# Values of one pair of blocks and scores of the next pair in one stage, at the ends of groups of units

## The chip, the cores and the metric

The kernel runs on one core of one Trainium2 chip. The metric is the device time of one execution in microseconds (us); the kernel before takes 741.47 us, the median of three runs (741.28 to 741.74).

A core has five engines, each with its own instruction queue: TensorE (PE in the profile; PEld is its weight load), VectorE (DVE), ScalarE (ACT), GpSimd (POOL) and SyncE (SP), which here issues the DMAs. They meet only through semaphores. TensorE writes its results to PSUM, eight banks of 128 x 512 fp32 each, and VectorE or ScalarE must read a bank out before it is written again.

## The reference

A retention block feeds a maxout feed-forward network (FFN):

```python
scores = scale * np.matmul(q, k.transpose(0, 1, 3, 2))        # 8 batches, 8 heads, 576 positions, 64 wide
Dmat = np.where(rel >= 0, gamma[:, None, None] ** rel[None, :, :], 0.0)
attn_out = np.matmul(scores * Dmat[None], v)                  # causal, with a decay per head, no softmax
x = attn_out.transpose(0, 2, 1, 3).reshape(B * S, H * D)      # 4608 tokens x 512
h = np.maximum(np.maximum(x @ w1, x @ w2), x @ w3)            # 512 x 768 each
out = h @ w_out                                               # 768 x 512
```

## The kernel before

**Tiles.** The 4608 tokens are 36 blocks of 128 (`g`, 0 to 35) and nine tiles of 512 (`t`, 0 to 8), four blocks to a tile. Because the decay has no softmax, retention is computed block by block with a running state per head: within a block scores and values, between blocks a 64 x 64 state for each head. From block 8 on (`BY_CHUNKS`) a block is cut into two halves of 64 tokens, so all its matmuls are 64 x 64 and four of them fit in the array at once.

**Retention of a pair of blocks.** For blocks a and b in turn:

- `load` (L244) issues the DMAs on SP: 8 for q and 8 for k in a layout for transposing (L240), then k and v as they lie (L258). `decay` (L260) queues eight scalings of v on ScalarE (L208), which the FFN's loop takes one by one with `scale`.
- `transposes` (L274) queues two VectorE transposes, of k and of q (shown at L213, the line of `chore`).
- `scores` (L297) first issues all that is queued, then calls `chunk_scores` (L369): matmuls `sk` (L376) and `kv` (L379) into two PSUM banks a block, four for a pair, from the pool `ps_r`, which has four. It queues the causal mask (L383) and the updates of the state (L391 to L397, with a GpSimd multiply at L393 between two of them).
- `values` (L444) calls `chunk_values` (L519): matmuls `o` (L526 from the masked scores, L533 from the state) into two banks, also from `ps_r`, and `chunk_output` queues the two VectorE multiplies that move them into `xT`. At the end of a tile of four blocks `sums_of_x` queues thirteen more VectorE sums, which the FFN of that tile needs.

"Queued" here means put in the Python list `urgent`. While `ffn` runs it issues one entry of it after each fourth matmul, and entries of `chores` (sums of weights, of hidden values) in between. What is issued then stands in the engine's own queue in that order.

**FFN of a tile.** From tile 1 on the FFN uses a bilinear scheme with fewer products. The hidden size is cut into three groups (`fp`). In `up` (L878) a group takes 20 products (`PRODUCTS`), each of two matmuls 128 x 128 x 256 (four records in the profile), summed in five chains A to E. A and B lie in the two banks of `ps_x`; E, C and D take the two banks of `ps_y` in turn. After a product `after` (L886) copies the bank on ScalarE (L890) and joins it to others on VectorE (L893, "joins"). The last four products of a group are D2 (the 17th), B6, A6 and A7; D2, B6 and A7 have three joins each, and A7's finish the hidden values `h` of the group.

After three groups, 120 matmul steps, the down phase runs 20 products (`DOWNS`), numbered here 1 to 20: in `downs` (L719) chains E and G share one bank of `ps_y`, I has the other, H and C share one of `ps_x`, F and D the other. First come ten VectorE sums of `h` (L573). Chain I (`di`) takes product 1 and every second or third one after it, and ScalarE copies its running sum out after most of them (L739). VectorE computes the totals (L573), which both free banks and give the results: y11 reads E's bank after product 7, y14 reads H's bank after product 11; G's product 13 and C's product 15 write to those banks next. Eight results of 128 x 256 leave through a pool of four buffers and a DMA each (L744).

**What sets the order.** The last loop of the kernel runs `ffn(t)` as a generator which yields twelve times: nine times in the three groups (each third of a group, so the third, sixth and ninth yields fall at the ends of groups), after the fourth and tenth down product, and at its end. `steps(t + 1)` lists what is issued of the next tile's retention before each yield; `at(n, ...)` puts an entry at place n, so place 3, 6 and 9 are ends of groups, and 10 lies inside the down phase:

```python
        for n in range(0, CPT, 2):
            a, b, m = CPT * t + n, CPT * t + n + 1, 6 * (n // 2)
            ...
            at(s, (scores, a), (scores, b), (load, b + 2))
            at(s + 1, (decay, a + 2))
            at(s + 2, (decay, b + 2))
            at(s + 3, (values, [a, b]), (transposes, a + 2), (load, a + 4))
```

So for each tile scores of the first pair stand at place 1, its values at 4, scores of the second pair at 7 and its values at 10. A "visit" below is one such stay of TensorE at the 64 x 64 matmuls, between large ones. "Call t" is `steps(t)`.

## Time and profile before

| | before |
|---|---|
| median of three runs | 741.47 us |
| the profiled execution, first to last instruction (span) | 739.6 us |
| TensorE busy | 734.1 us, 99% |
| VectorE busy | 576.1 us, 78% |
| ScalarE busy | 345.0 us, 47% |
| GpSimd busy | 33.8 us, 5% |
| granted TensorE clock, mean | 0.999 |
| one tile's FFN with the next tile's retention (355 to 433 us) | 78.0 us |
| in it: TensorE, VectorE, ScalarE busy | 78.0, 58.9, 36.2 us |
| waits of TensorE in its list | 2.2 us, at the start |

In rows of the timeline the first number is the start in us from the span's start, the second the time from the first start to the last end, then engine, line, operation, the tile written and the tiles read, partitions x elements, and how many instructions the row merges. A bracket gives idle time before it and what ended that. The ends of matmuls are modelled, so a stream of them is read by its starts. A row of waits names who waited for whom. An L2xx line of VectorE's work may be the line of the helper that issued it (L208 scalings, L213 entries of `urgent`).

### The profile page before, as it was taken

The page shows a single profiled execution, that of the slowest core. Times are in us where ns is not written, and L with a number is a line of the kernel's source. Part 1 is how long each engine was busy: PE and PEld are TensorE (multiplying, and loading weights), DVE is VectorE, ACT ScalarE, POOL GpSimd, SP SyncE. Part 2 cuts the span into 40 slices and gives each one's busy share as a digit, 9 for nine tenths or more (in the row PEclk, how much of TensorE's full clock was granted, in tenths as well). Part 3 has the DMA queues.
Part 4 walks back from the last instruction along what each step waited for, and adds up shares of the span by engine and source line. Part 5 has one row for each costly group of instructions (what it writes and reads, how often), then busy time and mean ns, then how long its engine had stood idle before and what let it go on. Part 6 is the DMA issues. An engine that isn't in the chain of part 4 may idle for free.

```text
span 739.6 us, 17315 instructions
## 1 busy us (share of the span) xinstructions
PE 734.1 (99%) x6948; PEld 605.8 (82%) x6948; DVE 576.1 (78%) x1066; ACT 345.0 (47%) x731; POOL 33.8 (5%) x42
## 2 busy tenths in 40 slices
PE   8999999999999999999999999999999999999998
PEld 7654556888888888888888888888888888888887
DVE  5998897999886895699668876787768966893676
ACT  4674824454245534544354525543455255424441
POOL 2000000102000100000000000000100010000000
PEclk9999999999999999999999999999999999999999
DMA  9999533415242515141424243332514151000001
GB/s 209 249 245 268 116 59 83 89 21 96 66 85 42 97 36 105 39 83 44 109 51 75 49 107 60 59 58 58 115 22 95 39 106 30 1 31 29 0 1 57
DMA packets 226640, 58.85 MB, mean 80 GB/s; under 512 B 207872, under 2 KB 225280, under 8 KB 226560
## 3 DMA queue, kind: packets, MB, share of 16 engines
q1 hardware_dynamic: 225584, 57.71, 35.8%
q8 instruction: 54, 0.88, 0.5%
q14 instruction: 26, 0.21, 0.1%
q10 hardware_dynamic: 976, 0.04, 0.1%
HBM read 48.27 MB, written 9.44 MB: 78 GB/s over the span
## 4 chain that ended last, share of the span: by engine, by line
PE 97%; SPq 1%; DMA 1%; DVE 0%; issue 0%
PE a L905 20%; PE b L905 17%; PE c L905 9%; PE up L930 8%; PE di L750 7%; PE d L905 6%; PE e L905 6%; PE dhc L750 5%; PE deg L750 3%; PE sk L376 3%; PE down L917 3%; PE o L526 2%; PE dfd L750 2%; PE o L533 2%; PE dx L657 1%; SPq L258 1%
## 5 line engine op out<-in xcount | busy, mean ns | idle before, releaser
L893 DVE TENSOR_TENSOR part<-part 128x512 f32<-128x512 f32 x168 | 117.8, 701 | 86.2 <-ACT part L890 83.6
L890 ACT COPY part<-b 128x512 f32<-128x512 f32 x120 | 70.4, 586 | 163.5 <-PE b L905 163.5
L893 DVE TENSOR_TENSOR h<-h,part 128x512 f32<-128x512 f32 x120 | 83.2, 693 | 24.5 <-ACT h L890 20.5
L890 ACT COPY part<-a 128x512 f32<-128x512 f32 x96 | 56.3, 586 | 51.6 <-PE a L905 51.1
L208 ACT ACTIVATE vraw<-vraw,gk 128x64 f32<-128x64 f32 x240 | 76.8, 347 | 0.1
L905 PE MATMUL b<-s,n 128*128 128x256 f32 x288 | 73.9, 379 | 0.0
L930 PE MATMUL up<-xT,w 128*128 128x512 f32 (+2 forms) x160 | 64.2, 554 | 0.0
L905 PEld LDWEIGHTS b<-s,n 128*128 128x128 f32 x288 | 54.7, 190 | 7.4
L930 PEld LDWEIGHTS up<-xT,w 128*128 128x128 f32 x160 | 28.5, 190 | 29.4 <-issue 26.3
L905 PE MATMUL c<-xT,w 128*128 128x256 f32 x192 | 51.2, 389 | 0.0
L739 ACT COPY k<-di 128x256 f32<-128x256 f32 x49 | 18.2, 372 | 68.4 <-PE di L750 43.4
L905 PE MATMUL d<-s,w 128*128 128x256 f32 x192 | 49.8, 380 | 0.0
L905 PE MATMUL a<-xT,w 128*128 128x256 f32 x192 | 49.3, 379 | 0.0
L905 PE MATMUL b<-xT,n 128*128 128x256 f32 x192 | 49.3, 379 | 0.0
L905 PE MATMUL a<-s,w 128*128 128x256 f32 x192 | 49.3, 379 | 0.0
L393 POOL TENSOR_TENSOR s<-s,gs_of 64x512 f32<-64x512 f32 x21 | 22.5, 1072 | 558.1 <-DVE s L391 441.7
L905 PE MATMUL e<-xT,w 128*128 128x256 f32 x192 | 45.4, 379 | 0.0
L905 PE MATMUL a<-xT,n 128*128 128x256 f32 x192 | 45.4, 379 | 0.0
L905 PEld LDWEIGHTS e<-xT,w 128*128 128x128 f32 x192 | 36.5, 190 | 5.4 <-issue 0.5
L905 PEld LDWEIGHTS a<-xT,w 128*128 128x128 f32 x192 | 36.5, 190 | 5.0
L905 PEld LDWEIGHTS a<-s,w 128*128 128x128 f32 x192 | 36.5, 190 | 5.0
L905 PEld LDWEIGHTS b<-xT,n 128*128 128x128 f32 x192 | 36.5, 190 | 5.0
(200 smaller groups left out, 1378.2 us busy)
## 6 DMA issues: line engine op xcount, KB each, us to landing
bits<-in_moe_w_dram SPq DMA_DIRECT2D x36, 256.0 KB, 5.7
kraw<-in_k_dram SPq DMA_DIRECT2D x32, 256.0 KB, 3.1
vraw<-in_v_dram SPq DMA_DIRECT2D x32, 256.0 KB, 3.5
qraw<-in_q_dram SPq DMA_DIRECT2D x224, 32.0 KB, 2.1
kxraw<-in_k_dram SPq DMA_DIRECT2D x224, 32.0 KB, 2.1
out_dram<-osb SPq DMA_DIRECT2D x56, 128.0 KB, 1.7
bits<-in_moe_w_out_dram SPq DMA_DIRECT2D x6, 512.0 KB, 4.9
qraw<-in_q_dram SPq DMA_DIRECT2D x7, 256.0 KB, 5.6
```

What stands on the lines that cost most here:

```text
L208: scaling.popleft()()
L376: nc.tensor.matmul(s[half(c), h, :], lhsT=kT[half(c), h, :], rhs=qT[half(c), h, :], start=True, stop=True)
L393: nc.gpsimd.tensor_tensor(new, new, factor, op=ALU.mult)
L526: nc.tensor.matmul(o[m][half(c), n, u, :], lhsT=vds[g][half(m), h, :], rhs=sts[g][half(m), h, :], start=n == 0 and u == 0, stop=place(g, m ...
L533: nc.tensor.matmul(o[m][half(c), n, u, :], lhsT=stacks[g][half(m), h, :], rhs=qks[g]["q"][half(m), h, :], start=False, stop=True, skip_gro ...
L739: nc.scalar.copy(place, a)
L750: nc.tensor.matmul(banks[chain], lhsT=hidden(h, order, b, late_ones)[:, e], rhs=late["V"][v][:, e], start=begins and e == 0, stop=chain no ...
L890: nc.scalar.copy(of[step], ps[step[0]][:])
L893: nc.vector.tensor_tensor(of[dst], a, b, op=op)
L905: nc.tensor.matmul(ps[chain][:, e, :], lhsT=factor(w, 2 * fp + e), rhs=xS[t][x], start=n == 1 and e == 0, stop=ends, skip_group_check=True)
L917: nc.tensor.matmul(b[:], lhsT=h[:, fb, m * P:(m + 1) * P], rhs=w_sb["out", fb], start=fb == blocks[0], stop=fb == blocks[-1])
L930: nc.tensor.matmul(ps[:, a:b], lhsT=w_sb[i, fb][:, dc * P:(dc + 1) * P], rhs=xT[t][:, dc, a:b], start=dc == 0 and a == 0, stop=dc == NDC - ...
```

## The change

The change adds `merged`, which issues the values of one pair and the scores of the next without large matmuls between; rewrites the lists for calls 2 to 8; lets `chunk_values` take its two banks from `ps_y` instead of `ps_r`; and issues the two output multiplies at once where it does. Values (two banks), and scores of a pair (four), then use six banks in one stage. In call 3 the first pair's scores still stand alone at place 1, and the merged stages at 6 and 9; in calls 4 to 8 they stand at 3 and 9. After the stage both blocks of the pair after next are loaded, at once and not through `urgent`. For tiles from 2 on the flush of both lists moves ahead of the ninth yield. Three buffer counts change: k as it lies, from three (and one beside them) to two (and two), transposed q in halves from three to four, and the tag it shares with early scores with it.

```diff
-            bufs = {"k": 3, "q": 2, "v": 4}[n]
-            pool, bufs = (raw0, 1) if n != "v" and g < BY_PE and g % (bufs + 1) == bufs else (raw, bufs)
+            extra = {"k": 2, "q": 1, "v": 0}[n]
+            pool, bufs = (raw0, extra) if g < BY_PE and g % (2 + extra) >= 2 else (raw, 2)
...
-                both[n] = att.tile([P, H, D], FP32, tag=tag, name=n + "T", bufs=2 if n == "k" else 3)
+                both[n] = att.tile([P, H, D], FP32, tag=tag, name=n + "T", bufs=2 if n == "k" else 4)
...
-    def chunk_values(chunks, t, i):
-        o = [ps_r.tile([P, 2, NP, D], FP32, tag="r", name="o") for _ in range(2)]
+    def merged(chunks, following, to_fetch):
+
+        chore(len(urgent))
+        scale(len(scaling))
+        chunk_values(chunks, *divmod(chunks[0], CPT), ps_y, "y")
+        for g in following:
+            if g < NG:
+                chunk_scores(g)
+        for g in to_fetch:
+            if g < NG:
+                load(g)
+
+    def chunk_values(chunks, t, i, pool=ps_r, tag="r"):
+        o = [pool.tile([P, 2, NP, D], FP32, tag=tag, name="o") for _ in range(2)]
...
-        chunk_output(o, chunks, t, i)
+        chunk_output(o, chunks, t, i, pool is ps_y)
...
-            soon(partial(nc.vector.tensor_tensor, x[:, :, :, m], o[m][:],
-                         gq[:, :, half(m)].unsqueeze(1).to_broadcast([P, 2, NP, D]), op=ALU.mult))
+            step = partial(nc.vector.tensor_tensor, x[:, :, :, m], o[m][:],
+                           gq[:, :, half(m)].unsqueeze(1).to_broadcast([P, 2, NP, D]), op=ALU.mult)
+            step() if now else soon(step)
...
                 count += 1
+                if count == total and t > 1:
+                    chore(len(urgent) + len(chores))
...
-        chore(len(urgent) + len(chores))
         if t == 1:
+            chore(len(urgent) + len(chores))
...
-        for n in range(0, CPT, 2):
...
+        if t == 2:
...
+            at(5, (values, [a, b]), (transposes, c), (load, e, "v"), (transposes, d))
+            at(7, (scores, c), (scores, d), (load, e, "k"), (load, f))
+            at(8, (decay, e))
+            at(9, (decay, f))
+            at(10, (values, [c, d]), (transposes, e), (load, g, "v"))
+            return todo
+        if t == 3:
+            at(0, (transposes, b))
+            at(1, (scores, a), (scores, b), (load, c, "k"), (load, d))
+            at(2, (decay, c))
+            at(3, (decay, d), (transposes, c))
+            at(4, (transposes, d))
+            at(6, (merged, [a, b], [c, d], [e, f]))
+            at(7, (decay, e), (decay, f))
+            at(8, (transposes, e), (transposes, f))
+        else:
+            at(1, (transposes, c))
+            at(2, (transposes, d))
+            at(3, (merged, [a, b], [c, d], [e, f]))
+            at(4, (decay, e))
+            at(5, (decay, f))
+            at(6, (transposes, e))
+            at(7, (transposes, f))
+        at(9, (merged, [c, d], [e, f], [g, h]))
+        at(10, (decay, g))
+        at(11, (decay, h))
```

Here a to d are the four blocks of the tile that call t prepares, e to h those of the tile after it.

More of the change, by code (lines that the diff above doesn't have):

```diff
@@ L309, in scores @@
         for j in range(2):
-            st = sts[g, j] = att.tile([C, NP, C], FP32, tag=f"m{j}", name="st", bufs=2 + j)
+            st = sts[g, j] = att.tile([C, NP, C], FP32, tag=f"m{j}", name="st", bufs=2 + 2 * j)
             soon(partial(nc.vector.tensor_tensor, st[:], s[j][:],
@@ L534, in chunk_values, with chunk_output @@
                                          rhs=qks[g]["q"][half(m), h, :], start=False, stop=True, skip_group_check=True)
-        chunk_output(o, chunks, t, i)
-    def chunk_output(o, chunks, t, i):
+        chunk_output(o, chunks, t, i, pool is ps_y)
+    def chunk_output(o, chunks, t, i, now=False):
         if i == 0:
@@ L1112, in at @@
             for step, *args in what:
-                if step is values:
+                if step in (values, merged):
                     if args[0][0] < NG:
-                        todo[n].append(partial(values, *args))
+                        todo[n].append(partial(step, *args))
                 elif args[0] < NG:
@@ L1134, in steps @@
             return todo
-        for n in range(0, CPT, 2):
-            a, b, m = CPT * t + n, CPT * t + n + 1, 6 * (n // 2)
-            first_pair = a == BY_CHUNKS
-            s = m + 2 if first_pair else m + 1
-            at(m - (n > 0), (transposes, b))
-            if first_pair:
-                at(m, (decay, b), (load, a + 2), (carry, a))
-            at(s, (scores, a), (scores, b), (load, b + 2))
-            at(s + 1, (decay, a + 2))
-            at(s + 2, (decay, b + 2))
-            at(s + 3, (values, [a, b]), (transposes, a + 2), (load, a + 4))
+        a, b, c, d = range(CPT * t, CPT * t + CPT)
+        e, f, g, h = range(CPT * t + CPT, CPT * t + 2 * CPT)
+        if t == 2:
+            at(0, (transposes, b), (decay, b), (load, c, "v"), (carry, a))
+            at(2, (scores, a), (scores, b), (load, c, "k"), (load, d))
+            at(3, (decay, c))
+            at(4, (decay, d))
+            at(5, (values, [a, b]), (transposes, c), (load, e, "v"), (transposes, d))
[24 more added lines that the diff above has]
+        at(11, (decay, h))
         return todo
```

## The prediction

> **What bounds the kernel now.** First the page's busy shares and the chain that ended last:

> ```profile
> PE 734.1 (99%) x6948; PEld 605.8 (82%) x6948; DVE 576.1 (78%) x1066; ACT 345.0 (47%) x731; POOL 33.8 (5%) x42
> PE 97%; SPq 1%; DMA 1%; DVE 0%; issue 0%
> ```

> TensorE sets the time and waits for nobody (its waits add up to 2.2 us, all at the start). So an edit gains only by making the stream of matmuls shorter, and loses wherever a matmul must wait. Next, the timeline of TensorE around one scores visit and one values visit:

> ```profile
> 359.95 1.03 PE L905 MATMUL a<-s,w 128*128 128x256 f32 x4
> 360.91 0.27 PE L376 MATMUL sk<-qT,kT 64*64 64x64 f32 x2
> ...
> 362.95 1.13 PE L905 MATMUL c<-xT,w 128*128 128x256 f32 x4
> 363.92 1.03 PE L905 MATMUL b<-s,n 128*128 128x256 f32 x4
> ...
> 374.28 1.89 PE L905 MATMUL e<-xT,w 128*128 128x256 f32 x8
> ...
> 379.46 1.03 PE L905 MATMUL a<-s,w 128*128 128x256 f32 x4
> 380.41 1.16 PE L526 MATMUL o<-m,vraw 64*64 64x64 f32 x64
> 381.39 1.11 PE L533 MATMUL o<-qT,s 64*64 64x64 f32 x64
> 382.44 1.13 PE L905 MATMUL c<-xT,w 128*128 128x256 f32 x4
> 383.40 1.03 PE L905 MATMUL b<-s,n 128*128 128x256 f32 x4
> ```

> Four large records (one product) follow each other every 0.863 us. The values visit begins 0.09 late (380.32 expected), c begins 2.12 after 380.32, and its four records take 0.96, not 0.863: a visit costs 2.22. A scores visit costs 2.14 + 0.10. I use 2.23 for both.

> Then VectorE across the end of a group, where 374.28 above is E of the next group:

> ```profile
> 372.50 2.15 DVE L893 TENSOR_TENSOR part<-part 128x512 f32<-128x512 f32 x3 [2.05 <-ACT part L890]
> 374.69 0.69 DVE L893 TENSOR_TENSOR h<-h,part 128x512 f32<-128x512 f32 x1
> 375.30 1.41 DVE L893 TENSOR_TENSOR part<-part 128x512 f32<-128x512 f32 x2
> 376.62 2.20 DVE L893 TENSOR_TENSOR h<-h,part 128x512 f32<-128x512 f32 x3
> 378.86 0.42 DVE L573 TENSOR_TENSOR h<-h 128x256 f32<-128x256 f32 x1
> ```

> This is the line to remember. Nine joins start when ScalarE has copied D2 and depend on each other, so VectorE finishes a group 4.54 us after TensorE has left it (378.82 against 374.28). Call the moment when TensorE leaves a group T. In a down phase (TensorE leaves at 413.25, last join ends at 417.79) it is 4.54 again. Today that tail costs nothing, because what TensorE starts with needs none of it.

> Last, VectorE's work in a down phase and in a scores stage, TensorE's product 15 of the down phase, and GpSimd:

> ```profile
> 421.43 1.28 DVE L213 TENSOR_TENSOR xT<-o,gq 128x512 f32<-128x512 f32 x2
> 426.56 0.42 DVE L573 TENSOR_TENSOR osb<-dhc,k 128x256 f32<-128x256 f32 x1
> ```

> ```profile
> 427.55 1.03 PE L750 MATMUL dhc<-v,h 128*128 128x256 f32 x4
> ```

> ```profile
> 440.31 0.69 DVE L383 TENSOR_TENSOR m<-sk,causal 128x512 f32<-128x512 f32 x1
> 441.03 1.41 DVE L391 TENSOR_TENSOR s<-kv,s 64x512 f32<-64x512 f32 x2
> 442.47 0.69 DVE L383 TENSOR_TENSOR m<-sk,causal 128x512 f32<-128x512 f32 x1
> ```

> ```profile
> 442.61 1.04 POOL L393 TENSOR_TENSOR s<-s,gs_of 64x512 f32<-64x512 f32 x1 [31.98 <-DVE s L391]
> ```

> Product 15 begins 0.57 after the subtraction y14 (426.56 + 0.42) that reads the bank it writes: the smallest slack there.

> **Part 1, visits saved.** In calls t = 3 to 8 (t is the call here) before has 24 visits, 24 x 2.23 = 53.5 us. After has one lone scores visit and 12 merged stages, 11 of them with scores. A merged stage enters and leaves once: 2.12 + 2.14 less 0.2 is 4.06 us from T to the next large product, which is then 0.10 slow. If nothing waited, 11 merges would save 11 x 0.3 = 3.3 us. Bounds: 0.2 each if the 0.1 before the first large product is not saved, so 2.2 to 3.3.

> [...]

> **Part 2, the wait that the merge adds.** The values now lie in the FFN's banks (ps_y). The next user of the first one is E of the next group (or chain I, the first product of the down phase), and it can start only when VectorE has multiplied that bank into xT. That multiply is issued at once, but behind the nine joins on an engine that takes its work in order. So: joins end T + 4.54; the multiply starts T + 4.58 (378.86) and takes 0.68 (half the pair above is 0.64; its group's mean is 0.682): T + 5.26; a release takes some 0.07 (the values end at 382.50, their multiply starts at 382.56): T + 5.35. TensorE was ready at T + 4.06. The second bank follows at T + 5.95, before its user needs it (C comes four products later, the third down product two later), so it is hidden.

> In the changed kernel's own order five stages (the first of t = 4 to 8) have one transpose of q among the nine joins, 0.63 more (two transposes in a row stood at 389.15 and 389.78): T + 5.98. The second stage of t = 3 has three there, and the last is the one its second block's scores need: those start at T + 4.54 + 1.9 = 6.45, take 1.0, and the down phase starts at T + 7.5. All queued behind the waiting matmul is TensorE's, so each wait counts in full.

> Sum: 6 x 5.35 + 5 x 5.98 + 7.5 = 69.5, plus the lone visit 2.23, less 53.5: **+18.2 us**, the saving of part 1 included. Bounds: with the transposes hidden and no release time 12 x 5.26 + 2.23 - 53.5 = +11.8; with the 0.1 slow product each time and another 1 us in t = 3, +20.4.

> **Part 3, the down phase.** Before, values stood after its fourth product and masks were done in the groups. Now the stage before it puts into VectorE's queue 13 sums of x, two masks and four state updates, drained two per product, ahead of the totals that free banks. From T: multiplies until 5.8; ten hidden sums, 3.72 (417.71 to 421.43): 9.5; 12 of the sums of x, ten of them 3.6 in the trace before plus two of 0.34: 13.8; y11 and the last sum of x: 14.5. Product 13 waits for y11 (14.2) but starts only at 5.35 + 12 x 0.863 = 15.7: hidden, 1.5 to spare. Then mask 0.6, two updates 1.4, mask; GpSimd's 1.04 starts 0.17 after the second update (442.44 to 442.61); two more updates end at 19.1; y14 0.4: 19.55. Product 15 would start at 5.35 + 14 x 0.863 = 17.4 and waits 2.1 us. That holds in four stages (t = 4 to 7); in t = 3, one update fewer, from 7.5, some 1.1. The last (t = 8) has no scores. Nothing in the trace before shows this wait; it is worked out from rows. Below: zero, if the masks cost less than the 2.1 (a gain is excluded: the products' own pace is unchanged). Above: 3 each if GpSimd also holds the first update. I take **+9.5**.

> **Part 4, loads.** Two blocks are loaded at once after each stage: 36 issues at some 0.49 (eight q rows took 3.94) instead of 18. The second block's v is issued after 16 of these, about T + 12.7, and lands 3.5 later (median): T + 16.3. ScalarE's first scaling of it stands ahead of the copy that product 16 waits for, which by part 3 starts at 20.4: hidden, 4 to spare; if product 15 didn't wait, 2 to spare. In t = 3 the transposes are late, so q loads only from T, v lands near 21.5 and product 16 waits about 0.7: **+0.7**, between 0 and 3. The output DMAs queue behind these loads on SP (to T + 13.3), still before y11's data (14.2). The buffers traded between pools (k 3 to 2, q 3 to 4) cost nothing while the scores free k a whole group ahead. The flush that moves ahead of the ninth yield issues the same entries after the same product: nothing. Call 2 keeps its four visits in their places; its loads move but v is still on chip two places (11.5 us) before its scaling, longer than 18 issues and a landing, so nothing; if it were late, ScalarE would hold the groups' copies.

> **Sum.** 18.2 + 9.5 + 0.7 = 28.4. The profiled execution spans 739.6; 768.0 after; the median 741.5 stands 1.9 over the span, so 769.9.

> [...]

> **Rivals.** (a) Only the stage's wait: y14 is in time because masks overlap better than in a chain. 741.5 + 11.8 to 20.4, so 753 to 762. For it: 442.47 shows a mask slipped between. Against: 4.6 us of work is put ahead of a row with 0.57 slack.
> (b) The second block's v comes later than T + 20, ScalarE stands still, and product 16 with it: +2 in five down phases, 780, when it is 2 us past the 4 in hand. For it: ScalarE scales in order; against: 4 us to spare.
> (c) Faster: the multiply gets ahead of the tail. If the last join ended by T + 3.3 (4.06 less 0.68 and 0.07), no stage would wait and 3.3 us were saved: 738. Against: 4.54 at both ends shown, and a chain of nine joins that the change leaves as it is.
> (d) Wait and saving cancel, 741: would need joins ending near T + 3.6.

> **Numbers.** Forecast 0.70, (a) 0.14, (b) 0.10, (c) 0.04, (d) 0.02. The likeliest time is 770. The range 756 to 781 takes in most of (a) and (b). A difference of 0.2% (1.5 us) is about what a measurement of this kernel can tell. Faster 0.04, same 0.02, slower 0.94.

> **What would show it.** Right: E and the first down product start 5.3 to 6 after the last a of a group, released by VectorE's xT; product 15 released by osb<-dhc some 2 us late; some 21 + 10 us of waits in TensorE's list, 13 visits instead of 24. Wrong: TensorE waits for nobody, or its wait names ScalarE or a DMA. The prediction breaks if the joins do not run back to back after a stage.

## The result, and the profile after

The changed kernel takes 775.68 us (median of 5 runs, 774.95 to 776.76) against 741.58 us for the kernel before (5 runs, 741.28 to 741.74): a ratio of 1.046, 95% interval 1.0448 to 1.0474. Forecast were 770 us, with a range of 756 to 781. The profiled execution spans 774.0 us, 34.4 more than before. The page's busy shares and the chain that ended last, of the changed kernel:

```profile
PE 738.6 (95%) x6948; PEld 610.4 (79%) x6948; DVE 580.9 (75%) x1066; ACT 344.3 (44%) x731; POOL 34.0 (4%) x42
PE 79%; DVE 14%; DMA 2%; issue 1%; SPq 1%; ACT 1%; POOL 0%; DVEq 0%; POOLq 0%; ACTq 0%
```

TensorE issues the same 6948 matmuls, but VectorE now holds 14% of the chain, and TensorE's busy share went from 99 to 95%. What it waits for (columns: total us, number of waits, longest us):

```profile
PE dhc L763 <- DVE osb L586: 8.2, 4, 2.1
PE di L763 <- DVE xT L556: 4.4, 3, 3.0
PE di L763 <- ACT k L752: 4.4, 2, 3.7
PE kv L379 <- issue: 4.3, 5, 1.1
PE sk L376 <- issue: 3.3, 3, 1.5
PE sk L376 <- DVE qT L213: 3.2, 1, 3.2
PE e L918 <- DVE xT L556: 2.7, 4, 1.6
```

The first line is the forecast's part 3, lines two and seven are its part 2. Lines four and five were not foreseen: in eight stages TensorE stands still in the middle of the small matmuls, and the profile names nothing that it waits for. They lie beside the wait of part 2 and are hidden by it in this kernel (the stages with such a gap are as long as those without one); the experiments bring them out.

The end of a group, on TensorE and on VectorE (timeline; start, us, engine, line, operation, shape, count):

```profile
428.69 1.24 PE L918 MATMUL a<-xT,n 128*128 128x256 f32 x5
434.98 1.13 PE L763 MATMUL di<-w_out,h 128*128 128x256 f32 x4 [1.16 <-DVE xT L556]
```

```profile
432.12 2.21 DVE L906 TENSOR_TENSOR h<-h,part 128x512 f32<-128x512 f32 x3
434.24 1.28 DVE L556 TENSOR_TENSOR xT<-o,gq 128x512 f32<-128x512 f32 x2
```

T is 428.69 + 5 x 0.2158 = 429.77 (large matmuls follow each other every 0.2158 us, a quarter of a product). The multiply starts 4.47 after T and the first down product 5.21 after T. From T to the next large product, the twelve stages take, in order, 5.21, 7.44 (t = 3), 5.67, 5.21, 5.67, 5.21, 5.67, 5.21, 5.68, 5.21, 5.67 and 5.21 us: 67.1 together, 69.5 forecast.

The down phase of t = 5, on VectorE and TensorE:

```profile
443.44 0.41 DVE L586 TENSOR_TENSOR osb<-deg,k 128x256 f32<-128x256 f32 x1
...
444.11 0.68 DVE L383 TENSOR_TENSOR m<-sk,causal 128x512 f32<-128x512 f32 x1
444.82 1.41 DVE L391 TENSOR_TENSOR s<-kv,s 64x512 f32<-64x512 f32 x2
446.26 0.69 DVE L383 TENSOR_TENSOR m<-sk,causal 128x512 f32<-128x512 f32 x1
447.47 1.41 DVE L391 TENSOR_TENSOR s<-kv,s 64x512 f32<-64x512 f32 x2 [0.52 <-POOL s L393]
448.91 0.42 DVE L586 TENSOR_TENSOR osb<-dhc,k 128x256 f32<-128x256 f32 x1
```

```profile
446.31 1.03 PE L763 MATMUL di<-w_out,h 128*128 128x256 f32 x4
449.39 1.13 PE L763 MATMUL dhc<-v,h 128*128 128x256 f32 x4 [2.05 <-DVE osb L586]
450.36 1.48 PE L763 MATMUL di<-v,h 128*128 128x256 f32 x4
451.63 1.92 PE L763 MATMUL dfd<-w_out,n 128*128 128x256 f32 x4
```

Masks and state updates stand between y11 (443.44) and y14 (448.91), as worked out, and product 15 waits 2.05 us. The last two rows show something else: these products take 1.3 to 1.7 us instead of 0.863. The clock had fallen. The same in t = 3, where ScalarE stood behind a v that had not landed:

```profile
282.89 0.35 ACT L208 ACTIVATE vraw<-vraw,gk 128x64 f32<-128x64 f32 x1 [4.96 <-DMA vraw<-in_v_dram]
```

```profile
278.84 1.06 PE L763 MATMUL dhc<-v,h 128*128 128x256 f32 x4
283.55 2.08 PE L763 MATMUL di<-v,h 128*128 128x256 f32 x4 [3.65 <-ACT k L752]
```

Busy times by stretch, with the granted clock behind POOL's column:

```profile
283.55:286.95 3.40, 3.40 (x8) 2.77 (x9) 0.43 (x1) 1.29 (x5) 0.00 (x0) 0.50 0.03 9
286.95:289.00 2.05, 2.05 (x11) 1.80 (x11) 0.87 (x3) 0.89 (x4) 0.00 (x0) 1.00 0.18 64
```

The clock records have 0.5 from 283.54 for 3.41 us and from 450.79 for 3.41 us; each costs some 1.7 us. Where the 34.4 us went: stages 67.1 + 12 x 0.1 + 2.23 - 53.5 = 17.0. The down phases of t = 4, 6 and 7 take 19.78 where 17.37 is their length without waits (that of t = 8), so 2.41 for product 15 each, in t = 5 as well, 9.6 together. t = 5's takes 21.38, 1.6 more for the clock; t = 3's takes 23.98, of which 4.9 are waits (4.4 by the list) with what follows them, and 1.7 the clock. That is 34.8, with 0.4 too much.

### The profile page after: what moved, and what is told of

The parts are those of the page before. It is cut to its first block, busy times and chain, and to the rows that moved or that the text cites. A ratio compares the mean times of both kernels' runs of the same rounds, so it can differ in the third digit from the quotient of the medians.

```text
span 774.0 us, 17305 instructions
## 1 busy us (share of the span) xinstructions
PE 738.6 (95%) x6948; PEld 610.4 (79%) x6948; DVE 580.9 (75%) x1066; ACT 344.3 (44%) x731; POOL 34.0 (4%) x42
## 4 chain that ended last, share of the span: by engine, by line
PE 79%; DVE 14%; DMA 2%; issue 1%; SPq 1%; ACT 1%; POOL 0%; DVEq 0%; POOLq 0%; ACTq 0%
PE a L918 17%; PE b L918 15%; PE c L918 8%; PE up L943 8%; PE e L918 6%; PE d L918 5%; PE di L763 5%; DVE part L906 4%; PE dhc L763 3%; DVE h L906 3%; PE down L930 3%; PE deg L763 2%; DVE s L586 2%; PE dfd L763 1%; PE dx L670 1%
## 5 line engine op out<-in xcount | busy, mean ns | idle before, releaser
L208 ACT ACTIVATE vraw<-vraw,gk 128x64 f32<-128x64 f32 x240 | 75.5, 346 | 16.4 <-DMA vraw<-in_v_dram 16.3
L918 PEld LDWEIGHTS b<-s,n 128*128 128x128 f32 x288 | 54.8, 190 | 7.3
L918 PE MATMUL c<-xT,w 128*128 128x256 f32 x192 | 49.5, 380 | 0.0
L393 POOL TENSOR_TENSOR s<-s,gs_of 64x512 f32<-64x512 f32 x21 | 23.0, 1094 | 563.5 <-DVE s L391 538.4
L918 PEld LDWEIGHTS a<-xT,n 128*128 128x128 f32 x192 | 36.5, 190 | 4.9
```

The source lines that it names most:

```text
L208: scaling.popleft()()
L393: nc.gpsimd.tensor_tensor(new, new, factor, op=ALU.mult)
L918: nc.tensor.matmul(ps[chain][:, e, :], lhsT=factor(w, 2 * fp + e), rhs=xS[t][x], start=n == 1 and e == 0, stop=ends, skip_group_check=True)
```

## The experiments

The main theory: each part of the loss is an engine that takes its work in order and has something else ahead of what TensorE needs, so each goes when the order is mended. The rival: a merged stage is slow for itself. The edits below are against the changed kernel unless said otherwise; none leaves out a part of the computation.

**Copies by ScalarE, so that VectorE's joins free no bank.**

```
-            step() if now else soon(step)
+            src = o[m]
+            if now:
+                src = ppool.tile([P, 2, NP, D], FP32, tag="part", name="oc")
+                nc.scalar.copy(src[:], o[m][:])
+            soon(partial(nc.vector.tensor_tensor, x[:, :, :, m], src[:], ...))
```

> ScalarE copies each bank of a merged stage's values to SBUF; VectorE multiplies from there, later, and TensorE's next large product waits for ScalarE instead of VectorE's joins. My theory (the stage waits cost what the joins cost, 67.0 us in 12 stages in the changed kernel): the first large product can come at T + 4.06, 12 stages take 12 x 4.06 = 48.7 at the most favourable, so 18 less than 67.0; that is 758 to 759 us. If the gaps of 0.6 to 1.5 us without a named releaser that nine stages of the changed kernel show (8.6 us together) are a floor of their own, they stay: some 766 to 767. Rival (the stage is slow for itself, and the wait on VectorE only the last name in it): no change, 775 to 776. The waits of product 15 in the down phases (8.2 us) and the fall of the clock in two of them should stay in either theory, since the multiplies now come later in VectorE's queue, or get longer by up to 1 us each.

Measured: 766.88 us (765.31 to 768.38), 1.0336 of before (1.0316 to 1.0356). The time is that of the case with a floor. No large product waits for xT any more, and what remains in the stages is this (its waits of TensorE):

```profile
PE kv L379 <- issue: 5.7, 5, 1.2
PE sk L376 <- DVE qT L213: 3.2, 1, 3.2
PE sk L376 <- issue: 3.1, 3, 1.4
```

These are eight gaps, 8.8 us together; in the changed kernel they are eight as well, 7.6 us by lines four and five of its list, not nine and 8.6. Two stages without a gap take 3.98 from T to the next large product; the forecast had 4.06 for a stage that waits for nobody. The eight with a gap take 4.85 to 5.65, and t = 3's second, which waits for qT, 8.25. So part 2's cause is right for the first product's wait, but the forecast's saving without that wait, 3.3 us, is not to be had: another floor stands just below. The sum of the stages fell by 5.2 (67.1 to 61.9), less than the 9 or 10 expected; the rest of the 8.8 us came from t = 3's wait for ScalarE (4.4 to 2.1) and from product 15 (8.2 to 6.2), less what the clock took back: 13.65 us at half clock in this profile (mean clock 0.991), 6.82 in the changed kernel's (0.996).

**Masks of the second stage held until the down phase is over.**

```
     def soon(step):
-        if spread:
+        if holding:
+            held.append(step)
+        elif spread:
...
+            urgent.extend(held)      (after the down phase)
+            held.clear()
```

> The masks and state updates of each second merged stage are kept out of VectorE's queue until the down phase is over. My theory: product 15's wait for y14 goes (8.2 us in four down phases), and with it the half clock in the down phase of t = 5 (1.7 us, 3.41 us at 0.5): 775.7 - 8.2 - 1.7 = 765.8. The 4.4 us that products 10 and 16 of t = 3 wait for ScalarE stay, and so does the half clock there. Rival (GpSimd or the next wait behind it holds the same product, or the held work makes the next group's values late): 772 to 778.

Measured: 773.38 us (771.4 to 775.67), 1.0432 (1.0403 to 1.0461): a miss. Product 15's wait is gone altogether, as expected, but most of its 9.6 us were taken over. ScalarE and TensorE in the same down phase:

```profile
446.90 0.35 ACT L208 ACTIVATE vraw<-vraw,gk 128x64 f32<-128x64 f32 x1 [2.06 <-DMA vraw<-in_v_dram]
```

```profile
447.56 1.13 PE L770 MATMUL di<-v,h 128*128 128x256 f32 x4 [0.78 <-ACT k L759]
```

The second block's v lands at T + 18.5 (446.90 - 428.36; in the changed kernel 448.30 - 429.77, the same), not at T + 16.3 as forecast. The 2 us to spare behind product 15 were not there: three down phases wait 0.50 to 0.78 for ScalarE. The held work also moves into the next group, puts a second transpose among the joins there, and four first stages take 6.26 instead of 5.67. And the clock fell three times in its profile (mean 0.993), not twice (0.996). Two of the four runs took 771.4 us at a mean clock of 0.993, two 775.3 and 775.7 at 0.989 and 0.987, so part of the miss is the clock's.

**Scaling of v later.**

```
+            at(0, (decay, d))
...
-        at(10, (decay, g))
-        at(11, (decay, h))
+        at(11, (decay, g))
```

> ScalarE's scaling of the two blocks' v is put later (first block one place, second block into the next call). My theory: in the down phase of t = 3 ScalarE no longer stands behind the v that is still on its way, so products 10 and 16 lose their waits of 0.72 and 3.65 us, and the half clock that follows (1.7 us) goes; product 15 of t = 3 then waits for y14 by up to 1.1, as forecast. 775.7 - 4.4 - 1.7 + 1.1 = 770.7, without the last term 769.6. Rival (the transposes that came late make t = 3 slow, whatever ScalarE does): 775 to 776.

Measured: 770.71 us (770.26 to 774.34), 1.0406 (1.0382 to 1.0429). TensorE waits for ScalarE in no down phase, which shows the cause; that the time is the expected one to 0.1 us is luck. The clock fell twice all the same (mean 0.996): at 264.12, behind the 3.16 us that t = 3's second stage waits for qT (the stage takes 8.26 instead of 7.44), and in t = 5's down phase as before. Product 15 of t = 3 has no wait, where the forecast had put 1.1: with the half clock the phase began that much later, and y14 ends at 278.39, product 15 begins at 278.98.

**The three together.**

> The three edits together: copies out by ScalarE, masks held, scalings later. My theory, all three causes additive: 775.7 - 18 - 9.9 - 6.1 = 741 to 742 without a floor in the stages, and 738 if every merge then also gives its 0.3 us; with the 8.6 us of gaps as a floor 746 to 750. Rival (something else carries part of the 34 us): over 752.

Measured: 754.18 us (752.14 to 755.45), 1.0169 (1.0151 to 1.0188). The three edits alone took 8.8, 2.3 and 5.0 off, 16.1; together 21.5, since ScalarE no longer takes over what the masks give up and the clock does not fall once in this profile (mean 1.0). It is 4 to 8 us over the expectation, and by its own condition (over 752) the rival is right: something else carries a part. What TensorE still waits for shows what, 7.3 us of unnamed gaps and 4.1 of waits for qT:

```profile
PE kv L383 <- issue: 5.3, 5, 1.6
PE sk L380 <- DVE qT L213: 4.1, 3, 3.2
PE sk L380 <- issue: 2.0, 3, 1.1
```

**The price of a visit** (this one against the kernel before; the modes in its expectation are TensorE's work on 128 x 128 and on 64 x 64 tiles, 128*128 and 64*64 in the rows):

```
-            at(s, (scores, a), (scores, b), (load, b + 2))
-            at(s + 1, (decay, a + 2))
+            at(s, (scores, a), (load, b + 2))
+            at(s + 1, (scores, b), (decay, a + 2))
```

> The kernel before, with the scores of each pair's two blocks in two visits a place apart (14 more visits of TensorE to small matmuls, nothing else added). It measures the price of a visit by itself, on which the 3.3 us of the forecast's saving rests: 0.09 ahead, 0.10 on the first large product and 0.1 more each. My theory: 14 x 0.3 = 4.2 us more, 745.6. Rival (a visit costs nothing, the modes overlap): 741.4; rival (a visit costs more, since an interval in other rows hides it): over 748.

Measured: 756.6 us (756.12 to 756.79), 1.0203 (1.0188 to 1.0219). The time missed, the price did not: a visit of one block takes 1.18 from T, of two blocks 2.12, so another visit costs 0.24 and the slow product behind it 0.1: 14 x 0.34 = 4.8. The other 10 us were not expected. 6.2 of them are waits by its list of waits, which the later masks make in five down phases. The list is short because it goes by modelled ends. By the starts of large matmuls, the time by which they follow each other later than 0.2158 is 15.7 us in all after 120 us, and 3.9 in the kernel before; 10.1 of the difference lie in the down phases (product 15 comes 1.43 late in four of them, where its row says 1.27), and 1.7 elsewhere, most of it the slow products of the visits. With 14 x 0.24 this makes 15.2 of the 15.3 us. One of the waits (TensorE, then VectorE):

```profile
272.63 1.03 PE L750 MATMUL di<-w_out,h 128*128 128x256 f32 x4
274.92 1.13 PE L750 MATMUL dhc<-v,h 128*128 128x256 f32 x4 [1.27 <-DVE osb L573]
```

```profile
274.45 0.42 DVE L573 TENSOR_TENSOR osb<-dhc,k 128x256 f32<-128x256 f32 x1
```

Product 15 behind y14 again, here from one mask more: the smallest slack of the kernel before, 0.57, is what breaks first.

**What the unnamed gaps are.** The page counts 54 transfers on the queue of instructions:

```profile
q8 instruction: 54, 0.88, 0.5%
```

That is 16 KB each. Numbering TensorE's 13,968 records (weight loads, matmuls, and some 70 of its sequencer) in the order in which they start, every unnamed gap in a merged stage ends at a record that is 193 beyond a multiple of 256 (once, a second short one at 194), in every kernel that has such gaps; in the changed kernel all eight do, at the records 4545, 6081, 6849, 7617, 10177, 10945, 11713 and 12481. An estimate from these counts: 54 transfers of 16 KB for 13,968 records are 63 B a record. If 256 records fill one transfer, 64 B each, the 13,968 make 54.6 of them. In the three together (t = 3's second stage, which waits for qT and has no gap, left out):

| stage begins at (us) | record, beyond a multiple of 256 | gap (us) |
|---|---|---|
| 235.1 | 109 | 0.54 |
| 299.4 | 18 | 1.61 |
| 340.0 | 84 | 0.88 |
| 379.8 | 119 | 1.13 |
| 419.8 | 154 | none |
| 458.4 | 189 | none |
| 497.8 | 223 | 0.67 |
| 537.3 | 2 | 0.38 |
| 577.2 | 36 | 0.79 |
| 616.9 | 71 | 1.29 |

A merged stage has 480 records (the second in the table 512; in the others a batch begins or ends, which leaves 32 out) and uses 256 of them in 2.05 us. At the eight gaps of the changed kernel the time from one such boundary to the next is 2.90 to 3.69 us: a transfer of 16 KB begins 0.35 to 1.27 us after the one boundary, takes 0.88 to 1.22, and TensorE goes on 1.28 to 1.49 after it has landed. In its two stages that have scores and neither a gap nor a wait for qT, which begin at 155 and 190 beyond a multiple, a transfer begins 0.98 and 1.59 ahead of the boundary, and the 256 records take 2.05 and 1.87. To test it, 64 records were put at the start of everything:

```
+        if n == 6:
+            for _ in range(16):
+                nc.tensor.matmul(ps[:, :16], lhsT=spreader[:, 0, :], rhs=spreader[:, 0, :16], ...)
```

> The three edits together, with 16 matmuls of 16 columns more in the warming at the very start (64 records of TensorE more: weight loads and matmuls). Theory: the gaps without a named releaser in the merged stages are TensorE's own instructions that are not there yet: in every kernel so far each of them ends at a record of TensorE's stream whose number is 193 beyond a multiple of 256, which is 16 KB at 64 B, and only the stages that begin 154 and 189 beyond a multiple have none. So with 64 records more the gaps must again end at 193 beyond a multiple (64 records earlier in the work), the stages that began at 154 and 189 (at 419.8 and 458.4 us) begin at 218 and 253 and get a gap of 0.4 to 0.9 us, and those that began at 109, 84 and 119 (at 235.1, 340.0 and 379.8 us, gaps of 0.54, 0.88 and 1.13) begin at 173, 148 and 183 and lose it. The sum of the gaps stays about what it was, so does the time: 750 to 756. Rival (loads of data, banks or a semaphore make the gaps): they stay in the same stages, at the same matmul of each.

Measured: 760.11 us (757.2 to 761.46), 1.0246 (1.0219 to 1.0273). The time is off because the 16 matmuls delay the start by 6.5 us (the first scores visit of call 2 comes at 137.99 instead of 131.44), which I had left out. The gaps moved: all eight end at 193 beyond a multiple again, 64 records earlier in the work. The stages that begin at 173 and 183 have none now (0.54 and 1.13 before), the one at 253 has 0.50 (none before). Two came out only in part: the one at 148 keeps 0.64 of 0.88, and the one at 218 gets 0.24, just behind its end. With the 154 above, this puts the edge between 148 and 154. The page now counts one transfer more, as 64 records more would need (14,032 make 54.8):

```profile
q8 instruction: 55, 0.90, 0.5%
```

The rows with an idle time in the stage that begins at 119, before the shift:

```profile
384.01 0.27 PE L380 MATMUL sk<-qT,kT 64*64 64x64 f32 x2 [1.13 <-issue]
```

and in the two stages that begin at 183 and 253, after it:

```profile
390.08 0.33 PE L383 MATMUL sk<-qT,kT 64*64 64x64 f32 x3 [0.45 <-DVE qT L216]
...
468.60 0.33 PE L383 MATMUL sk<-qT,kT 64*64 64x64 f32 x3 [0.46 <-DVE qT L216]
470.13 0.27 PE L383 MATMUL sk<-qT,kT 64*64 64x64 f32 x2 [0.50 <-issue]
```

The rival, gaps that stay at the same matmul, falls.

**The transposes of t = 3 earlier.** First as a mere change of place:

```
-            at(7, (decay, e), (decay, f))
-            at(8, (transposes, e), (transposes, f))
+            at(7, (transposes, e))
+            at(8, (decay, e), (decay, f), (transposes, f))
```

> The three edits together, with the q transposes of the first block of t = 3's second stage put one place earlier, so that VectorE's queue ahead of that stage holds one block's less. In the three edits together the scores of that stage still wait 3.16 us for qT, and the stage takes 7.44 us. My theory: the wait shrinks to nothing or to what one transpose costs (0.6), the stage takes 4.0 to 5.3: 2 to 3 us off, 751 to 752 against 754.2. Rival (q itself is not on chip in time, its eight DMAs are issued behind others): no change, or slower by up to 3 us where ScalarE stands.

Measured: 754.55 us (753.06 to 756.06), 1.0177 (1.016 to 1.0193), no change. It tested nothing: the small work is handed out at a fixed rate, the masks stood ahead, and VectorE's order came out the same. Then with the transposes put ahead of the masks:

```
+    def ahead(g):
+        rest = list(urgent)
+        urgent.clear()
+        transposes(g)
+        urgent.extend(rest)
+        chore(2)
...
+            at(7, (ahead, e))
+            at(8, (ahead, f), (decay, e), (decay, f))
```

> The three edits together, and the four transposes of t = 3's second stage taken to the front of VectorE's queue of small work (the earlier try left that queue's order as it was). The stage's wait of 3.16 us for qT should go; what is left of it is the gap for instructions, which here comes at the stage's second boundary (the stage begins 239 beyond a multiple of 256). My theory: the stage takes 4.7 to 5.0 instead of 7.44, 2.5 us off: 751.5 to 752 against 754.2 to 754.6. All merged stages then stand at 4.06 plus gaps; together they take 58.5, the visits of before 51.3, so it stays some 7 us and more over before. Rival (the transposes wait for q itself, which lands late): no change, and VectorE's joins behind them are late too, up to 757.

Measured: 750.24 us (749.47 to 751.46), 1.0123 (1.0106 to 1.0139). The stage takes 5.00 instead of 7.44, and the gap that was to appear there did, at record 5313 = 20 x 256 + 193:

```profile
262.32 0.21 PE L387 MATMUL sk<-qT,kT 64*64 64x64 f32 x1 [0.71 <-issue]
```

This is the fastest form of the merge found, and it is 9.1 us over before. Its twelve stages take 59.3; eleven at 3.98 and the last, without scores, at 2.88 would be 46.7. The 12.6 between is the price of the gaps (8.5 by their rows) and of two waits of 0.45 for qT (each gap costs some 0.3 more than its row says, as the matmul ahead of it has a modelled end that reaches into it). Without it the kernel would come out near 738, an estimate that no run shows.

**Values and scores apart again, the scores' loads and the scalings a place later with them, all else as in the last version.**

```
+    def followed(following, to_fetch):        (the scores and loads of merged)
...
             at(3, (merged, [a, b], [c, d], [e, f]))
+            at(4, (followed, [c, d], [e, f]))
...
         at(9, (merged, [c, d], [e, f], [g, h]))
+        at(10, (followed, [e, f], [g, h]))
```

> The version with all four edits, but values and scores apart again: the values of a pair alone at the end of a group, the scores of the next pair one place later (two places in t = 3, where q's transposes need it), loads and scalings behind them. It undoes the back-to-back issue alone and keeps banks, buffers, copies by ScalarE and held masks. Theory (a run of 512 records of TensorE's outruns the loading of its instructions, one of 256 does not): the unnamed gaps (8.5 us in ten stages) go altogether. In their place come 11 visits at 0.3 (3.3 us) and, as the lone last values visit of that version shows, 0.69 us on each of 11 more first products that wait for ScalarE's copy, which the scores no longer hide (7.6 us): 750.2 - 8.5 - 0.9 + 3.3 + 7.6 = 751.7. Rival (the gaps belong to the place, the banks or the loads): they stay, and the time is 760.

Measured: 770.45 us (770.05 to 773.0), 1.0406 (1.0384 to 1.0427). A miss in time: at the end of t = 3 TensorE waits 12.7 us for a VectorE that stands behind a transpose I had placed ahead of its q. But there is not one unnamed gap in it. So once more with t = 3's first stage left merged:

> The same as the try before, but with t = 3's first stage left back to back and the transposes for its second stage in their old places, since there VectorE stood 12.7 us at the end of t = 3 behind a transpose whose q was still on its way (a place that I had chosen badly, and that says nothing on the theory). Ten of the eleven merges are undone. Theory: the gap of 0.54 us of t = 3's first stage is the only unnamed one left; 10 visits at 0.3 and ten first products 0.69 to 0.81 late behind ScalarE's copy come in place of 8.0 us of gaps and 0.9 for qT: 750.2 - 8.0 - 0.9 + 3.0 + 7.3 = 751.6; the try before, less its 12.7 us, less 1.8 more at its 257.8 and less two stretches at half clock (3.4), would be 768.0 - 17.9 = 750.1 of span and 752 of time. Rival (the gaps belong to the place, the banks or the loads): 758 to 760, with gaps.

Measured: 753.8 us (751.55 to 754.92), 1.0154 (1.0135 to 1.0174). TensorE's waits:

```profile
PE di L782 <- ACT oc L573: 5.0, 6, 2.0
PE e L937 <- ACT oc L573: 4.0, 5, 0.8
PE warm L175 <- DVE inf L614: 1.1, 1, 1.1
PE sk L387 <- issue: 1.1, 1, 1.1
```

One unnamed gap is left, in the one stage that is still merged. With the same banks and copies, and the same loads at most two places later, the gaps go when a run of 480 or 512 records becomes two of 224 or 256. What comes in their place, ScalarE's copy that no scores hide any more (9.0 us) and ten visits more, costs somewhat more than they did.

## Why the prediction was right

The time lies 5.7 us above the 770 and inside the range; the sign, the bound and the order of the causes came out as forecast. The sum of 28.4 became 34.4.

- **Part 2, the stage's wait for xT**: 17.0 against 18.2. Six stages were put at 5.35 and take 5.21, five at 5.98 and take 5.67 to 5.68, one at 7.5 and takes 7.44. In the six, the last join ended at T + 4.55 as forecast, but the multiply began 0.08 before that end, at T + 4.47 instead of 4.58, and one transpose cost 0.47 rather than 0.63. (5.26 and 0.07 for the release make 5.33, not 5.35; the release took 0.055.) The copies by ScalarE show the cause: without the joins ahead of it, the wait is gone.
- **Part 1, the saving of 3.3 us** assumed that a merged stage runs at the pace of a visit. The price of a visit is right (0.34 against 0.3), the length without gaps is right (3.98), but with the xT wait gone only two stages of eleven have it. Hidden under part 2 here; it decides as soon as part 2 is mended. This step was wrong in its premise, and that it cost the forecast nothing was luck.
- **Part 3, product 15**: waits of 2.03 to 2.06 against 2.1, in the four stages named; with what follows each 9.6 against 8.4, the forecast's 9.5 without t = 3. The 1.1 in t = 3 did not come, since ScalarE held that phase earlier. Holding the masks removes the wait; the next one in line is ScalarE, 1.3 to 1.6 us behind.
- **Part 4, loads**: the mis-sized term. t = 3's down phase lost 6.6 us, 1.7 of it to the clock, where 0.7 here and 1.1 in part 3 were put. The second block's v was put at T + 21.5 and landed at T + 24.7 or so; product 16 waited 3.65 instead of 0.7, and product 10 another 0.72 for the first block's. In the other calls v lands at T + 18.5, not 16.3, 3.5 after its issue as forecast: it was issued at T + 15.0 in t = 5, not T + 12.7, since two of the issues ahead of it took 1.44 and 1.73 us instead of some 0.49. "4 to spare" was 2 at best. The mechanism of rival (b) was closer than its chance of 0.10 said.
- **The clock** stood in no term and cost 3.3 us: two stretches at 0.5 of 3.41 us each, one behind a wait of 3.65 us and one behind a wait of 2.05. The profile before, with a mean clock of 0.999, has no wait above 1.1 us and could show neither.

Rival (a) falls with the 8.2 us of product 15; (c) and (d) with the xT waits. No version beat the kernel before. With the named waits down to 1.6 us (the last merged version), the unnamed gaps take more (8.5 us by the rows) than the eleven merges save (11 x 0.34 = 3.7), and the drift of mostly 34 or 35 records from one stage to the next lets only one or two in seven begin in a good place.

## What to carry to other kernels

Before two bursts of work are put back to back, list what each in-order engine has ahead of the operation that frees the bank, and add it up from the moment TensorE leaves: here this gave the waits for xT to 0.3 us and the four of product 15 to within 0.1, but neither of the two in t = 3's down phase, which hung on when a load lands. When a wait is mended, look for the next one in line before counting the gain; of 9.6 us the held masks gave back only 2.3. And count records, not only time: here merged 64 x 64 matmuls used 256 records in 2.05 us where nothing held them, and 2.90 to 3.69 us passed over 256 records where TensorE stood, so beside a saving of 0.3 us for each merge came 0.6 to 1.5 us of standing still in eight stages.

## What the runs showed of the hardware

The clock fell twice inside the changed kernel's profile, each time to 0.5 for 3.41 us, at 283.54 and at 450.79: 167.25 us apart, 49 times 3.413. Cut into stretches of 3.413 us from 283.54 on, both ways, TensorE is idle (by modelled ends) for all of the 3.41 us just ahead of the first fall and for 2.01 us of those just ahead of the second; after 120 us, the kernel's end left out, no other stretch has more than 1.72. So the length of a wait did not decide here. Of the four waits of product 15 (2.03 to 2.06 us) the one that ended at 449.39 was followed by a fall; the wait of 3.17 us for qT that ended at 264.51, which the stretches cut into 1.72 and 1.45, was not, nor was the one of 3.02 us that ended at 684.29, cut into 1.63 and 1.39. A wait of 2 us cost 1.7 us more in one place and nothing in three others. That the clock goes by such stretches is a reading of this one profile; no run tests it.
